# One ring of seven PSUM banks, value products of 6, 5 and 5 key tiles, and maxima turned by a matmul, in an attention and MLP kernel

## The chip, the cores and the metric

The kernel runs on one core of a Trainium2 chip. Five engines work beside each other and wait for each other through semaphores: TensorE (PE, matmuls; PEld is its loading of stationary operands), VectorE (DVE), ScalarE (ACT), GpSimd (POOL), and SyncE (SP), which issues the DMAs. Matmul results go to eight PSUM banks, each 128 partitions of 512 float32 numbers, from which DVE and ACT read them. The metric is the device time of one execution in microseconds (us); lower is better.

## The reference

```python
xn  = layernorm(x)                                   # x: 2048 x 1024
q, k, v = heads(xn @ wqkv)                           # 32 heads of 32 columns
p   = softmax(q @ k.T * 32 ** -0.5)                  # 2048 x 2048 for each head
s   = merge(p @ v) @ wo                              # 1024 x 1024
h   = xn @ w1 + b1                                   # 3584 columns
g   = silu((h * tanh(softplus(h))) @ w2)             # Mish between two dense layers
out = x + s * g
```

All of it is float32. The kernel splits most operands into a high and a low part in the type fp32r and takes three products (high by high, high by low, low by high); the products of softmax weights and values are in plain float32.

## The kernel before, in words

There are three stages. The first (to about 580 us) normalises `x`, makes values, queries and keys, and splits the MLP's weights. The third (from about 3295 us) is the output projection `op` (`p_mm`, L1073) with the end of the formula. Between them lies the long stage that the change is about, in which attention and MLP are woven into one another.

For each head, key tile `T` (128 keys, 16 to a head) and 512 queries, a matmul `t` (L748) makes scores with the row's maximum already subtracted: the stacked operands `qstack` and `kstack` hold three copies of 32 rows for the split, and two further rows of `qstack` hold the negated maximum as a high and a low part. ACT takes the exponential into an SBUF tile `p` (L756). POOL adds the 16 `p` tiles of a head one after the other into `z` (L777). TensorE multiplies them by the values (`pv`, L795) in four 32-column strips of its array, which gives all 2048 queries in one bank. Finally four matmuls `zp` (L818) sum `z` over its partitions, and `norm` divides.

The maxima come from another pass of the same scores, about five key tiles ahead: matmul `s` (L670), DVE's `reduce_max` `mx` (L676). After four query tiles `m_chain` (L686) reduces (`nm`), splits into high and low (`hl`, ACT then POOL), turns the 128x8 result by a TensorE transpose into 8x128 (`mtp`, L700), copies it to `mt` on ACT and has SP store it into `qstack` with two DMAs. A `t` waits for that.

The MLP supplies matmuls `h` (L893, 24 for one tile of 128 hidden columns by 512 rows) and `y` (L981, six to a bank), with a chain of ACT and DVE operations for Mish between them and DVE's additions `yacc` (L1001).

The engines' orders are written ahead of time by `Plan` (L74), which walks through the stage with durations of its own (`MM`, `PV` and the number in each `Op`), takes for each engine the ready operation with the lowest key, and emits it. `ring` objects stand for buffers: an operation may only be taken when each ring in its `take` has a free place. Banks are in fixed rings: `s` has two, `t` two (the turned maxima use these too), `d` three (`h`, `y`, Mish's `q` and `zp`), `o` one (`pv`). `p` has 5 tiles. An operation with `late` may be taken as soon as it is ready while TensorE is in column mode (`col`, its strips or the narrow transpose), and that many us later otherwise.

In words, a *visit* is below a run of TensorE instructions in strip form between instructions that use the whole array.

Of the kernel before, what the change touches and what calls it, by code (L numbers as in the profile page):

```python
# [9 lines left out]
F32 = mybir.dt.float32  # L10
# [52 lines left out]
class Op:  # L63


    def __init__(self, eng, took, need=(), emit=None, take=(), give=(), key=None, col=False, late=0.0,
                 bytes_=0, then=None, first=False, both=False):
        self.eng, self.took, self.need, self.emit = eng, took, need, emit
        self.take, self.give, self.key, self.col, self.late = take, give, key, col, late
        self.bytes, self.then, self.first, self.both = bytes_, then, first, both  # L70
        self.end = None


class Plan:  # L74
# [6 lines left out]
    SEM, SWITCH, LAND, RATE = 0.07, (0.2, 0.1), 2.0, 0.25e6  # L81
# [53 lines left out]
    def do(self, op, when):  # L135
# [27 lines left out]
    def run(self, streams):  # L163
        self.streams = [[s, None] for s in streams]
        while True:
# [5 lines left out]
            for e in sorted(left, key=self.at.get):  # L171
                now, best, soon = self.at[e], None, None
                for op in self.todo[e] + (heads if e == "PE" else []):
# [5 lines left out]
                    if "d" in op.take and not op.first and len(self.rings["d"]) == 1 and self.first_of("d"):  # L179
                        continue  # L180
# [3 lines left out]
                    key = (not op.late, r if op.key is None else op.key)  # L184
# [21 lines left out]
def body(ctx: ExitStack, tc: tile.TileContext, x, wqkv, wo, w1, b1, w2, out):  # L206
# [25 lines left out]
    make_identity(nc, ident)  # L232
    bias1 = consts.tile([P, FT], F32, name="bias1")
# [268 lines left out]
    stacks(early, 1)  # L502
    vt = {}

# [28 lines left out]
    def m_tail(h, g, mx):  # L533
        nm = early.tile([P, 4], F32, tag=f"nm{g % 2}", name=f"nm{h}_{g}")
        hl = early.tile([P, 2, 4], F32R, tag=f"hl{g % 2}", name=f"hl{h}_{g}")
# [9 lines left out]
        def r3():  # L545
            tp = ps1.tile([P, 512], F32, tag="ps", name=f"mtp{h}_{g}")
            nc.tensor.transpose(tp[:8, :P], hl.bitcast(F32).rearrange("p a b -> p (a b)"), ident)
            copy(mt, tp[:8, :P])
# [111 lines left out]
    def s_stream():  # L660
        for h in range(1, H):
            while h not in loaded:
                yield None
            for g in range(4):
                maxes, tiles = [], {}
                for qt in range(4 * g, 4 * g + 4):
                    for kc in range(4):
                        def mm(at, h=h, qt=qt, kc=kc, tiles=tiles):
                            tiles[qt, kc] = sp_ = bank("s", at["s"], f"s{h}_{qt}_{kc}")
# [3 lines left out]
                        def mx(at, h=h, g=g, qt=qt, kc=kc, tiles=tiles):  # L673
                            if qt == 4 * g and kc == 0:
# [4 lines left out]
                               emit=mm, take=["s"])  # L679
                        yield m  # L680
                        maxes.append(op("DVE", 0.69, need=[m] + maxes[:1], emit=mx, give=[("s", m)],
# [4 lines left out]
    def m_chain(h, g, maxes, tiles, late=LATE):  # L686
# [4 lines left out]
        def r2(at):  # L691
            tiles["hl"] = early.tile([P, 2, 4], F32R, tag=f"hl{at['hl']}", name=f"hl{h}_{g}")
            copy(tiles["hl"][:, 0], tiles["nm"])

        def r3(at):
            low(nc.vector if h == 0 else nc.gpsimd, tiles["hl"][:, 1], tiles["nm"], tiles["hl"][:, 0])

        def r4(at):
            tiles["tp"] = tp = bank("t", at["t"], f"mtp{h}_{g}")
            nc.tensor.transpose(tp[:8, :P], tiles["hl"].bitcast(F32).rearrange("p a b -> p (a b)"), ident)  # L700
# [13 lines left out]
        a = op("PE", 0.06, need=[a], emit=r4, take=["t"], give=["hl"], col=True, late=late)  # L714
        a = op("ACT", 0.28, need=[a], emit=r5, take=["mt"], give=[("t", a)])
# [3 lines left out]
    exps, adds, uses = {}, {}, {}  # L719
    vt_, pv, zs = {}, {}, {}  # L720
# [13 lines left out]
    def t_stream():  # L734
        pts = {}
        for T in range(NS):
# [4 lines left out]
            for c in range(4):  # L741
# [4 lines left out]
                def mm(at, T=T, c=c, h=h, kt=kt, tile_=tile_):  # L746
                    tile_[0] = tp = bank("t", at["t"], f"t{T}_{c}")
# [8 lines left out]
                m = Op("PE", MM, key=slot * (T + (c + 1) / 4), emit=mm, take=["t"],  # L756
                       need=[m_there[h, c]] if (h, c) in m_there else [])
                yield m
                exps[T].append(op("ACT", 0.69, need=[m] + exps[T][:1], emit=ex, take=["p"] if c == 0 else [], give=[("t", m)]))
# [8 lines left out]
            if kt % GROUP == GROUP - 1:  # L768
                product(T, pts)
# [17 lines left out]
    def product(T, pts):  # L787
        h, kt = divmod(T, NT)

        def emit(at):  # L790
            if kt == GROUP - 1:
                pv[h] = bank("o", 0, f"pv{h}")
            for k in range(kt - GROUP + 1, kt + 1):
# [4 lines left out]
        def then(o):  # L798
            for k in range(T - GROUP + 1, T + 1):
                p_done(k, o)  # L800

        need = [e for k in range(T - GROUP + 1, T + 1) for e in exps[k]]
        last_pv[h] = op("PE", PV * GROUP, key=slot * (T + 1.5), need=need + [vt_[h]], emit=emit, col=True,
                        take=["o"] if kt == GROUP - 1 else [], give=["v"] if kt == NT - 1 else [], then=then)
# [3 lines left out]
    def norm(h, product_, sum_):  # L808
# [6 lines left out]
        def z_mm(at):  # L815
            t["z"] = bank("d", at["d"], f"zp{h}")
# [26 lines left out]
        a = own = op("PE", 1.0, need=[sum_], emit=z_mm, take=["d"], give=["z"], col=True, late=LATE)  # L843
# [4 lines left out]
        a = op("DVE", 0.69, need=[a, oc], emit=n3, give=[("d", own)])  # L848
# [30 lines left out]
    def h_stream():  # L879
        for n in range(NC * FT):  # L880
# [7 lines left out]
            for k in range(KT):  # L888
                for a, b in THREE:
                    def mm(at, n=n, c=c, k=k, a=a, b=b, i=i, t=t):  # L890
                        if i == 0:
                            t["h"] = bank("d", at["d"], f"h{n}")
# [5 lines left out]
                           take=["d", "h"] if i == 0 else [],  # L898
# [8 lines left out]
    def mish(n, made, t):  # L907
# [9 lines left out]
        def a2(at):  # L917
            t["q"] = bank("d", at["d"], f"q{n}")
# [34 lines left out]
        p2 = op("ACT", 0.69, need=[p1], emit=a2, take=["d"], first=True)  # L953
# [5 lines left out]
        o5 = op("DVE", 0.69, need=[o4], emit=d5, give=[("d", p2)])  # L959
        o6 = op("DVE", 0.69, need=[o5, o3], emit=d6, give=["r"])  # L960
        p5 = op("ACT", 0.6, need=[o6], emit=a5, take=["act"])
        act_ops[n] = op("DVE", 0.69, need=[p5], emit=d7, give=[("d", t["own"]), "h"])
# [3 lines left out]
    def y_stream():  # L966
        for m in range(W2S):
            w2_op(m, [m_there[0, 3]])
        for B in range(NC * FT // YB):
            c, b = divmod(B, FT // YB)  # L970
            done = []
            for dh in range(2):
                for s in range(4):
                    t = {}
                    for j in range(YB):
                        n, m_ = YB * B + j, (B * 2 + dh) * YB + j
                        for i, (p, q) in enumerate(THREE):
                            def mm(at, n=n, m_=m_, p=p, q=q, s=s, i=i, j=j, dh=dh, B=B, t=t):
                                if j == 0 and i == 0:
                                    t["y"] = bank("d", at["d"], f"y{B}_{dh}_{s}")  # L980
# [4 lines left out]
                            while n not in act_ops or m_ not in w2_ops:  # L985
# [3 lines left out]
                                   need=[act_ops[n], w2_ops[m_]], take=["d"] if j == 0 and i == 0 else [], give=give)  # L989
# [12 lines left out]
                    done.append(op("DVE" if b else "ACT", 0.69 if b else 0.6, emit=y_add, give=[("d", t["own"])],  # L1002
# [67 lines left out]
    BANKS = ("s0", "s1", "t0", "t1", "d0", "d1", "d2", "o0")  # L1070
# [8 lines left out]
    def p_stream():  # L1079
# [31 lines left out]
        for part in range(2):  # L1111
            for n, name in enumerate(BANKS):
                t, dh = divmod(n, 2)
                need = {"s": "s", "t": "s", "d": "y" if name < "d2" else "z", "o": "z"}[name[0]]
                while need not in final:
                    yield None
                need = [final[need]] + ([last_t[H - 1]] if name[0] == "t" else [])
                for k in range(FIRST) if part == 0 else range(FIRST, KT):
                    for i in range(3):
                        def mm(at, t=t, dh=dh, k=k, i=i, name=name):  # L1120
                            if k == 0 and i == 0:
                                ps[t, dh] = bank(name[0], at[name[0]], f"op{t}_{dh}")
                            p_mm(t, dh, k, i)
                        yield Op("PE", MM, key=2 * total, need=need + [wo_ops[k], o_ops[k]], emit=mm,
                                 take=[name[0]] if k == 0 and i == 0 else [])
# [5 lines left out]
    m_chain(0, 3, [], {"mx": negm[0]}, late=0.0)  # L1131
# [49 lines left out]
    for c in range(NC):  # L1181
        for s in range(4):
# [3 lines left out]
            for dh in range(2):  # L1186
# [5 lines left out]
                if c:  # L1192
                    n = 2 * s + dh
                    ps[t, dh] = bank(BANKS[n][0], int(BANKS[n][1]), f"op{t}_{dh}")
# [38 lines left out]
```

## Time and profile before

| | |
|---|---|
| median of 3 runs | 3469.94 us (3468.89 to 3470.29) |
| the profiled execution | 3472.93 us, of which the span is 3471.2 us |
| PE busy | 3438.9 us, 99% |
| DVE, ACT, POOL busy | 2356.7, 1982.8, 2471.5 us |
| granted TensorE clock, mean | 0.999 |
| the woven stage | about 581 us (first `t`) to 3295 us (last `y`) |

A busy PE here isn't a TensorE that starts a matmul at every chance: a 128x512 matmul is recorded as 389 ns or more, while the next may start 227 ns after it. Where the distance from start to start is over 227 ns but the record still covers it, TensorE has lost time without an idle time being shown. So the profile is read below by starts and counts.

### The profile page before, as it was taken

What the parts mean: (1) busy time and instruction counts of PE and PEld (TensorE: products, weight loads), DVE (VectorE), ACT (ScalarE), POOL (GpSimd) and SP (SyncE); (2) the same over time, 40 slices, a digit from 0 to 9 for tenths busy, and PEclk for the clock granted to TensorE, in tenths of its full rate; (3) what the DMA queues carried; (4) which work ended last, traced back from release to release, by engine and by line L of the source; (5) the groups of instructions that cost most, each with busy time, mean ns of one, the idle gap of its engine ahead of it and who ended that gap; (6) DMA issues with size and microseconds to landing.
All of it is one profiled execution on the core that took longest, in us unless ns stands there. A gap on an engine that the chain in (4) does not pass through costs nothing.

```text
span 3471.2 us, 48388 instructions
## 1 busy us (share of the span) xinstructions
PE 3438.9 (99%) x17920; PEld 2519.7 (73%) x17920; DVE 2356.7 (68%) x3839; ACT 1982.8 (57%) x3298; POOL 2471.5 (71%) x846
## 2 busy tenths in 40 slices
PE   8999999999999999999999999999999999999999
PEld 8998887666666767677666676776666766766687
DVE  6012236877877777887887778778878788776533
ACT  6111112766666667666666667666666666667621
POOL 0654342788787878888878878888888788888800
PEclk9999999999999999999999999999999999999999
DMA  8898896433333354443343544343445433333382
GB/s 290 291 306 304 287 321 208 122 110 99 122 110 110 106 162 125 119 122 98 110 114 118 158 123 121 110 116 104 121 117 178 120 117 113 110 115 117 122 303 85
DMA packets 294192, 529.79 MB, mean 153 GB/s; under 512 B 88810, under 2 KB 147178, under 8 KB 270186
## 3 DMA queue, kind: packets, MB, share of 16 engines
q1 hardware_dynamic: 274100, 484.74, 45.1%
q10 hardware_dynamic: 19856, 41.95, 3.3%
q8 instruction: 142, 2.33, 0.3%
q14 instruction: 94, 0.77, 0.1%
HBM read 386.89 MB, written 138.67 MB: 151 GB/s over the span
## 4 chain that ended last, share of the span: by engine, by line
PE 94%; POOL 2%; DVE 2%; ACT 1%; DMA 1%; issue 0%; SPq 0%; POOLq 0%; ACTq 0%; DVEq 0%
PE h L893 17%; PE y L981 17%; PE t L748 13%; PE s L670 13%; PE pv L795 13%; PE qk L598 10%; PE v L312 5%; PE op L1076 5%; POOL z L777 1%; PE zp L818 1%; PE mtp L700 1%; DVE mx L676 1%; ACT p L252 1%; PE s L525 0%; PE pt L367 0%
## 5 line engine op out<-in xcount | busy, mean ns | idle before, releaser
L777 POOL TENSOR_TENSOR z<-z,p 128x2048 f32<-128x2048 f32 x448 | 2065.2, 4610 | 115.0 <-ACT p L252 92.2
L252 ACT ACTIVATE p<-t,zero 128x512 f32<-128x512 f32 x2048 | 1382.4, 689 | 516.2 <-PE t L748 495.6
L676 DVE TENSOR_REDUCE mx<-s 128x1 f32<-128x512 f32 x1984 | 1329.8, 686 | 396.1 <-PE s L670 390.8
L981 PE MATMUL y<-w,act 128*128 128x512 f32 x2688 | 865.7, 393 | 2.6 <-DVE r L938 1.9
L748 PE MATMUL t<-qstack,kstack 128*128 128x512 f32 x2048 | 807.0, 397 | 5.0 <-ACT p L252 3.5
L670 PE MATMUL s<-kstack,qstack 128*128 128x512 f32 x1984 | 779.1, 396 | 5.0 <-DVE mx L676 2.8
L893 PE MATMUL h<-xr,w 128*128 128x512 f32 x2016 | 698.5, 391 | 0.6 <-DVE yacc L1001 0.3
L981 PEld LDWEIGHTS y<-w,act 128*128 128x128 f32 x2688 | 501.6, 188 | 118.1 <-issue 5.0
L748 PEld LDWEIGHTS t<-qstack,kstack 128*128 128x128 f32 x2048 | 384.1, 188 | 117.9 <-ACT p L252 17.2
L795 PE MATMUL pv<-p,v 128*32 128x512 f32 x4096 | 466.0, 595 | 0.0
L670 PEld LDWEIGHTS s<-kstack,qstack 128*128 128x128 f32 x1984 | 372.3, 188 | 109.3 <-DVE mx L676 19.6
L893 PEld LDWEIGHTS h<-xr,w 128*128 128x128 f32 x2016 | 377.8, 188 | 82.1 <-issue 2.8
L598 PE MATMUL qk<-xc,qkw 128*128 128x512 f32 x1536 | 350.9, 389 | 0.0
L777 POOL TENSOR_TENSOR z<-p,p 128x2048 f32<-128x2048 f32 x32 | 147.6, 4612 | 262.3 <-PE zp L818 193.4
L1001 DVE TENSOR_TENSOR yacc<-yacc,y 128x512 f32<-128x512 f32 x416 | 283.2, 681 | 73.9 <-PE y L981 73.1
L598 PEld LDWEIGHTS qk<-xc,qkw 128*128 128x128 f32 x1536 | 288.1, 188 | 59.9
L795 PEld LDWEIGHTS pv<-p,v 128*32 128x32 f32 x4096 | 120.0, 109 | 274.5 <-issue 265.9
L893 PE MATMUL h<-xc,w 128*128 128x512 f32 x672 | 237.3, 392 | 0.2 <-DVE yacc L1001 0.2
L263 DVE TENSOR_TENSOR qst<-qk,qst 128x512 fp32r<-128x512 f32 x64 | 44.3, 692 | 245.9 <-ACT qst L255 245.9
L255 ACT ACTIVATE qst<-qk 128x512 fp32r<-128x512 f32 x64 | 38.3, 598 | 299.2 <-PE qk L598 264.6
L312 PE MATMUL v<-vw,xc 128*128 128x256 f32 x1536 | 191.4, 286 | 2.2 <-POOL vw L263 1.5
L312 PEld LDWEIGHTS v<-vw,xc 128*128 128x128 f32 x1536 | 187.3, 193 | 3.8 <-POOL vw L263 1.9
(90 smaller groups left out, 2385.0 us busy)
## 6 DMA issues: line engine op xcount, KB each, us to landing
w<-w1s SPq DMA_DIRECT2D x112, 1024.0 KB
w<-w2s SPq DMA_DIRECT2D x224, 512.0 KB
w2s<-pw SPq DMA_DIRECT2D x56, 512.0 KB
qstack<-qs SPq DMA_DIRECT2D x96, 256.0 KB
kstack<-ks SPq DMA_DIRECT2D x96, 256.0 KB
w1s<-w1p SPq DMA_DIRECT2D x20, 1024.0 KB
praw<-in_B_w_dram SPq DMA_DIRECT2D x72, 256.0 KB
x<-in_A_x_dram SPq DMA_DIRECT2D x32, 512.0 KB
```

The source lines that it names most:

```text
L252: nc.scalar.activation(out_, in_, fn, bias=zero if bias is None else bias, scale=scale)
L312: nc.tensor.matmul(ps[:, :256], xc[t // 4][:, a, k, (t % 4) * P:(t % 4 + 1) * P], w[:, b, k], start=n == 0, stop=n == 3 * KT - 1)
L598: nc.tensor.matmul(ps, w[:, a, k], xc[c][:, b, k], start=n == 0, stop=n == 3 * KT - 1)
L670: nc.tensor.matmul(sp_, qst[h % 3][:, qt * P:(qt + 1) * P], kst[h % 3][:, kc * 512:(kc + 1) * 512], start=True, stop=True)
L676: nc.vector.reduce_max(tiles["mx"][:, qt % 4, kc:kc + 1], tiles[qt, kc], axis=AX.X)
L748: nc.tensor.matmul(tp, kst[h % 3][:, kt * P:(kt + 1) * P], qst[h % 3][:, c * 512:(c + 1) * 512], start=True, stop=True)
L777: nc.gpsimd.tensor_tensor(zs[h], pts[T - 1] if kt == 1 else zs[h], pts[T], ALU.add)
L795: nc.tensor.matmul(pv[h][c * DH:(c + 1) * DH, :], vt[h][:, k, :], pts[T - kt + k][:, c * 512:(c + 1) * 512], start=k == 0, stop=k == NT - 1)
L893: nc.tensor.matmul(t["h"], w1t[n][:, a, k], xts_[c][:, b, k], start=i == 0, stop=i == 3 * KT - 1)
L981: nc.tensor.matmul(t["y"], acts[n][:, p, s * P:(s + 1) * P], w2t[m_][:, q], start=j == 0 and i == 0, stop=j == YB - 1 and i == 2)
L1001: nc.vector.tensor_tensor(ya, ya, t["y"], ALU.add)
L1076: nc.tensor.matmul(ps[t, dh], ohl[t // 4, k][:, a, s * P:(s + 1) * P], wt[k][:, b, r], start=k == 0 and i == 0, stop=k == KT - 1 and i == 2)
```

## The change

- Seven banks are one ring `b`, which `s`, `t`, `h`, `y`, `q`, `zp` and `mtp` all take from. The old rings stay as limits: at most 2 `s`, 2 `t`, 4 `d` at a time. The eighth bank stays with `pv`.
- A head's value product is in three pieces of 6, 5 and 5 key tiles instead of four pieces of 4. The last also needs POOL's finished sum (`adds[T]`), so that `zp` can follow it in the same visit. The `p` ring grows from 5 to 7 tiles, the `act` ring shrinks from 4 to 3. 15 KB a partition of DMA scratch are given up.
- The maxima are turned by an ordinary matmul in fp32r: the stationary operand is a fixed 128x128 tile `hl` whose first 8 columns hold the values and whose others are zero, the moving operand a 128x128 identity. It is no longer in strip form, and has `late` 4.0.
- The planner's durations change (`MM` 0.231 to 0.228, `PV` 0.91 to 0.86, `SWITCH` 0.2 and 0.1 to 0.25 and 0.13), an engine's next start may lie a little ahead of an end (`AHEAD`), and maxima and `y` additions get offsets in their keys (`urgent`).

```diff
-MM, PV = 0.231, 0.91
+MM, PV = 0.228, 0.86
-GROUP, YB = 4, 2
+GROUPS, YB = (6, 5, 5), 2
-LEAD, LATE = 5, 8.0
+LEAD, LATE = 5, 4.0
-PS, ACTS, W2S, Y0, Y1 = 5, 4, 5, 0.6, 0.17
+PS, ACTS, W2S, Y0, Y1 = 7, 3, 5, 0.6, 0.17
+S_B, T_B, D_B = 2, 2, 4
+U_MX, U_Y = -2.0, 1.0
...
+    AHEAD = {"DVE": 0.08, "ACT": 0.1, "POOL": 0.0}
-    SEM, SWITCH, LAND, RATE = 0.07, (0.2, 0.1), 2.0, 0.25e6
+    SEM, SWITCH, LAND, RATE = 0.07, (0.25, 0.13), 2.0, 0.25e6
...
             op.end = start + took
+            took -= self.AHEAD[e]
...
-                    key = (not op.late, r if op.key is None else op.key)
+                    key = (not op.late, r - op.urgent if op.key is None else op.key)
...
+    hls = [early.tile([P, P], F32R, name=f"hl{i}") for i in range(2)]
+    for t in hls:
+        nc.vector.memset(t.bitcast(F32), 0.0)
+    def parts(i):
+        return hls[i][:, :8].rearrange("p (a b) -> p a b", a=2)
+    def turn(tp, i):
+        nc.tensor.matmul(tp[:, :P], hls[i], ident_r, start=True, stop=True)
...
-    for name, n in (("s", 2), ("t", 2), ("d", 3), ("o", 1), ("p", PS), ("z", 1), ("e", 1), ("r", 1), ("on", 1),
+    for name, n in (("b", 7), ("s", S_B), ("t", T_B), ("d", D_B), ("o", 1), ("p", PS), ("z", 1), ("e", 1), ("r", 1), ("on", 1),
...
-    def bank(ring, i, name):
-        return ps_a.tile([P, 512], F32, tag=f"{ring}{i}", name=name)
+    def bank(at, name):
+        return ps_a.tile([P, 512], F32, tag=f"b{at['b']}", name=name)
...
-                               emit=mm, take=["s"])
+                               emit=mm, take=["s", "b"])
...
         def r4(at):
-            tiles["tp"] = tp = bank("t", at["t"], f"mtp{h}_{g}")
-            nc.tensor.transpose(tp[:8, :P], tiles["hl"].bitcast(F32).rearrange("p a b -> p (a b)"), ident)
+            tiles["tp"] = tp = bank(at, f"mtp{h}_{g}")
+            turn(tp, tiles["hl"])
...
-        a = op("PE", 0.06, need=[a], emit=r4, take=["t"], give=["hl"], col=True, late=late)
+        a = op("PE", 0.07, need=[a], emit=r4, take=["t", "b"], give=["hl"], late=LATE if h else 0.0)
...
-            if kt % GROUP == GROUP - 1:
-                product(T, pts)
+            if kt in group_of:
+                product(T, pts, group_of[kt])
...
+        if kt == NT - 1:
+            need.append(adds[T])
...
-        a = own = op("PE", 1.0, need=[sum_], emit=z_mm, take=["d"], give=["z"], col=True, late=LATE)
+        a = own = op("PE", 1.0, need=[sum_], emit=z_mm, take=["d", "b"], give=["z"], col=True, late=LATE)
```

What TensorE does at the end of a head, here head 15. `pv` is the value product, `zp` the partition sums, `mtp` a turned maximum, `s17_5_0` a score matmul for the maxima of head 17 and `t256_1` one for the weights of key tile 256 (head 16). Before, the last piece of the product and then, 40 rows further on, the sums:

```order
L670 MATMUL s17_5_0_18601<-kstack2_5380,qstack2_5379 128x512
L795 MATMUL pv15_17985<-p252_18409,v15_17764 32x512 x4
L795 MATMUL pv15_17985<-p253_18467,v15_17764 32x512 x4
L795 MATMUL pv15_17985<-p254_18499,v15_17764 32x512 x4
L795 MATMUL pv15_17985<-p255_18549,v15_17764 32x512 x4
L700 MATMUL mtp17_0_18628<-ident_154,hl17_0_18557 8x128
L981 MATMUL y26_0_3_18630<-w2_104_17840,act52_18104 128x512 x3
```

```order
L748 MATMUL t258_1_18730<-qstack1_2723,kstack1_2724 128x512
L670 MATMUL s17_7_1_18732<-kstack2_5380,qstack2_5379 128x512
L981 MATMUL y26_1_2_18706<-w2_107_18292,act53_18435 128x512
L818 MATMUL zp15_18736<-z15_17957,ones_164 32x512 x4
L893 MATMUL h55_18532<-xr1_12077,w1_55_18316 128x512
L981 MATMUL y26_1_3_18748<-w2_106_18147,act52_18104 128x512
```

After, the last piece and the sums:

```order
L1007 MATMUL y26_1_1_18579<-w2_107_18223,act53_18322 128x512
L691 MATMUL s17_6_1_18606<-kstack2_5383,qstack2_5382 128x512
L818 MATMUL pv15_18039<-p251_18307,v15_17702 32x512 x4
L818 MATMUL pv15_18039<-p252_18352,v15_17702 32x512 x4
L818 MATMUL pv15_18039<-p253_18383,v15_17702 32x512 x4
L818 MATMUL pv15_18039<-p254_18433,v15_17702 32x512 x4
L818 MATMUL pv15_18039<-p255_18483,v15_17702 32x512 x4
L844 MATMUL zp15_18634<-z15_17860,ones_166 32x512 x4
L1007 MATMUL y26_1_1_18579<-w2_107_18223,act53_18322 128x512
L919 MATMUL h55_18468<-xr1_12054,w1_55_18247 128x512
L771 MATMUL t257_2_18645<-qstack1_2725,kstack1_2726 128x512
```

The last piece has five key tiles instead of four, waits for POOL's sum, stands later against the `t` of the next head, and the sums come in the same visit.

The turning of one maximum on TensorE, the third of head 15. Before:

```order
L748 MATMUL t232_0_17368<-qstack2_5379,kstack2_5380 128x512
L893 MATMUL h50_17357<-xr1_12077,w1_50_17091 128x512 x2
L795 MATMUL pv14_17142<-p228_17160,v14_16930 32x512 x4
L795 MATMUL pv14_17142<-p229_17236,v14_16930 32x512 x4
L795 MATMUL pv14_17142<-p230_17287,v14_16930 32x512 x4
L795 MATMUL pv14_17142<-p231_17332,v14_16930 32x512 x4
L700 MATMUL mtp15_2_17403<-ident_154,hl15_2_17339 8x128
L670 MATMUL s15_13_0_17405<-kstack0_2718,qstack0_2717 128x512
L748 MATMUL t232_1_17409<-qstack2_5379,kstack2_5380 128x512
```

After (with line 523 the helper `turn`):

```order
L691 MATMUL s15_14_1_17380<-kstack0_2720,qstack0_2719 128x512
L919 MATMUL h50_17310<-xr1_12054,w1_50_17038 128x512 x2
L523 MATMUL mtp15_2_17386<-ident_r_159,hl1_2728 128x128
L691 MATMUL s15_14_2_17388<-kstack0_2720,qstack0_2719 128x512
L919 MATMUL h50_17310<-xr1_12054,w1_50_17038 128x512 x2
L771 MATMUL t233_2_17398<-qstack2_5382,kstack2_5383 128x512
L771 MATMUL t233_3_17401<-qstack2_5382,kstack2_5383 128x512
```

The turned maximum used to stand at the end of a visit; now it stands among whole-array matmuls with a load of 128 columns of its own.

The end of the woven stage on TensorE, where `y55` is the MLP's last block and `op0_0` the first tile of the projection. Before, with the sums of the last head:

```order
L981 MATMUL y55_0_2_31744<-w2_220_31541,act110_31531 128x512 x3
L981 MATMUL y55_0_2_31744<-w2_221_31670,act111_31685 128x512 x3
L981 MATMUL y55_0_3_31753<-w2_220_31541,act110_31531 128x512 x3
L981 MATMUL y55_0_3_31753<-w2_221_31670,act111_31685 128x512 x3
L981 MATMUL y55_1_0_31762<-w2_222_31679,act110_31531 128x512 x3
L1076 MATMUL op0_0_31767<-wo0_30236,xo0_31621 128x512 x3
L1076 MATMUL op0_0_31767<-wo1_30967,xo0_31621 128x512 x3
L1076 MATMUL op0_0_31767<-wo2_31609,xo0_31621 128x512 x3
L1076 MATMUL op0_0_31767<-wo3_31616,xo0_31621 128x512 x3
L1076 MATMUL op0_1_31787<-wo0_30236,xo0_31621 128x512 x3
L818 MATMUL zp31_31792<-z31_31156,ones_164 32x512 x4
L981 MATMUL y55_1_0_31762<-w2_223_31720,act111_31685 128x512 x3
```

After, with its last value product:

```order
L1007 MATMUL y54_1_3_31554<-w2_219_31321,act109_31400 128x512 x3
L1103 MATMUL op0_0_31567<-wo0_30128,xo0_31503 128x512
L1007 MATMUL y55_0_0_31570<-w2_220_31338,act110_31438 128x512 x3
L1103 MATMUL op0_0_31567<-wo0_30128,xo0_31503 128x512 x2
L818 MATMUL pv31_31112<-p507_31271,v31_30821 32x512 x4
L818 MATMUL pv31_31112<-p508_31316,v31_30821 32x512 x4
L818 MATMUL pv31_31112<-p509_31387,v31_30821 32x512 x4
L818 MATMUL pv31_31112<-p510_31433,v31_30821 32x512 x4
L818 MATMUL pv31_31112<-p511_31459,v31_30821 32x512 x4
L844 MATMUL zp31_31607<-z31_30998,ones_166 32x512 x4
L1007 MATMUL y55_0_0_31570<-w2_221_31514,act111_31579 128x512 x3
L1007 MATMUL y55_0_1_31626<-w2_220_31338,act110_31438 128x512 x3
```

The sums of the last head (`zp31`) used to be alone between `op` and `y`; now the last product and they stand together, four `y` tiles earlier.

More of the change, by code (lines that the diff above doesn't have):

```diff
@@ L178, in run @@
                         r = max(r, self.at["POOL"])
-                    if "d" in op.take and not op.first and len(self.rings["d"]) == 1 and self.first_of("d"):
+                    if not op.first and any(x in op.take and len(self.rings[x]) == 1 and self.first_of(x) for x in "db"):
                         continue
@@ L232, in body @@
     make_identity(nc, ident)
+    ident_r = consts.tile([P, P], F32R, name="ident_r")
+    nc.vector.tensor_copy(ident_r, ident)
     bias1 = consts.tile([P, FT], F32, name="bias1")
@@ L684, in s_stream, with m_chain @@
         final["s"] = m
-    def m_chain(h, g, maxes, tiles, late=LATE):
+    def m_chain(h, g, maxes, tiles):
         def r1(at):
@@ L847, in norm @@
         a = op("DVE", 0.69, need=[a], emit=n2, give=["r"])
-        a = op("DVE", 0.69, need=[a, oc], emit=n3, give=[("d", own)])
+        a = op("DVE", 0.69, need=[a, oc], emit=n3, give=[("d", own), ("b", own)])
         stored[h] = op("SP", 0.4, need=[a], emit=store, give=["on"], bytes_=P * 512 * 4)
@@ L952, in mish @@
         p1 = op("ACT", 0.73, need=[o1], emit=a1)
-        p2 = op("ACT", 0.69, need=[p1], emit=a2, take=["d"], first=True)
+        p2 = op("ACT", 0.69, need=[p1], emit=a2, take=["d", "b"], first=True)
         o2 = op("DVE", 0.75, need=[p1], emit=d2)
@@ L988, in y_stream @@
                             m = Op("PE", MM, key=tile_time * due, emit=mm,
[L989 removed]
+                                   need=[act_ops[n], w2_ops[m_]], take=["d", "b"] if j == 0 and i == 0 else [], give=give)
                             if j == 0 and i == 0:
```

79 lines of the change are left out of this document (41 added, 38 removed).

## The prediction

> **What bounds the kernel now.** I read the page first (sections 1, 2 and 4), then the woven stage by windows, then the timeline where TensorE changes its way of working, then the table of waits.
>
> ```profile
> span 3471.2 us, 48388 instructions
> PE 3438.9 (99%) x17920; PEld 2519.7 (73%) x17920; DVE 2356.7 (68%) x3839; ACT 1982.8 (57%) x3298; POOL 2471.5 (71%) x846
> PEclk9999999999999999999999999999999999999999
> PE 94%; POOL 2%; DVE 2%; ACT 1%; DMA 1%; issue 0%; SPq 0%; POOLq 0%; ACTq 0%; DVEq 0%
> ...
> 700.00:3200.00 2500.00, 2491.55 (x12861) 1734.09 (x12850) 1967.32 (x3177) 1672.37 (x2761) 2076.68 (x567) 1.00 0.40 119
> 700.00:3200.00 2500.00, 432.17 (x3804) 111.14 (x3792) 1.00 0.40 119
> 700.00:3200.00 2500.00, 30.89 (x232) 4.56 (x232) 1.00 0.40 119
> 700.00:3200.00 2500.00, 32.20 (x118) 9.81 (x118) 1.00 0.40 119
> ```
>
> TensorE carries 94% of the chain that ended last, with its clock granted at 0.9 or more in every slice. The four window rows are the stretch from 700 to 3200 us for everything, then for line 795 (`pv`), 818 (`zp`) and 700 (`mtp`) alone. So 12861 - 3804 - 232 - 118 = 8707 whole-array matmuls run there. What they need at least comes from these rows, of the chain and the timeline:
>
> ```profile
> 482.53 5.44 PE qk L598 x24
> 1099.40 0.13 PEld L795 LDWEIGHTS pv<-p,v 128*32 128x32 f32 x4 [0.30 <-issue]
> 1099.83 0.13 PEld L795 LDWEIGHTS pv<-p,v 128*32 128x32 f32 x4 [0.30 <-issue]
> ...
> 2201.52 0.39 PE L893 MATMUL h<-xr,w 128*128 128x512 f32 x1
> 2201.84 3.64 PE L795 MATMUL pv<-p,v 128*32 128x512 f32 x32
> 2205.41 0.73 PE L670 MATMUL s<-kstack,qstack 128*128 128x512 f32 x2
> ...
> 1353.20 0.61 PE L981 MATMUL y<-w,act 128*128 128x512 f32 x2
> 1353.75 1.06 PE L818 MATMUL zp<-z,ones 128*32 128x512 f32 x8
> 1354.74 0.50 PE L893 MATMUL h<-xr,w 128*128 128x512 f32 x1
> ...
> 1507.50 3.64 PE L795 MATMUL pv<-p,v 128*32 128x512 f32 x32
> 1511.07 0.27 PE L700 MATMUL mtp<-ident,hl 128*8 128x128 f32 x1
> 1511.10 0.48 PE L748 MATMUL t<-qstack,kstack 128*128 128x512 f32 x1
> ```
>
> A dense whole-array matmul costs 5.44 / 24 = 0.227 us; four strip instructions cost 0.43 us, so a key tile (eight) 0.86. A visit costs more than its content: from `h` at 2201.52 to `s` at 2205.41 are 3.89 us; less 0.227 for `h` and 8 x 0.43 = 3.44 for the product, 0.22 is left for the two changes of form. The `zp` visit, with its second `y` 0.227 after 1353.20, says the same: 1.31 - 0.227 - 0.86 = 0.22. A turned maximum at the end of a visit takes 0.03 (1511.07 to 1511.10).
>
> Sum for the stretch: 8707 x 0.227 = 1976; strips 4036 / 4 x 0.43 = 434; visits, 165 by the order of the whole stage and so some 153 here, x 0.22 = 34; 118 turned maxima x 0.03 = 4. That is 2448 of 2500 us. The other 52 us are waits, most too short to show as idle time (2500 - 2491.55 = 8.5 us). Over the whole stage I take 60.
>
> ```profile
> PEld s L670 <- DVE mx L676: 19.6, 42, 0.9
> PEld t L748 <- ACT p L252: 17.2, 42, 1.0
> ...
> 1500.38 0.39 PE L670 MATMUL s<-kstack,qstack 128*128 128x512 f32 x1
> 1500.81 0.69 DVE L676 TENSOR_REDUCE mx<-s 128x1 f32<-128x512 f32 x1 [0.61 <-PE s L670]
> ```
>
> The loads of `s` and `t` wait for the reader of the bank that they are to fill. From a matmul's start to its bank's release are 0.43 + 0.69 = 1.12 us, five matmul steps of 0.227. A bank refilled after five steps or fewer makes TensorE wait, one refilled after six barely doesn't.
>
> **The change, part by part.** *Visits.* In the order, 165 visits become 96: 32 fewer products, the sums inside the last, no maxima in strips. 69 x 0.22 = 15.2 us gained; the content of the visits is the same 512 key tiles.
>
> *Turned maxima.* 125 of them in the stage cost 0.03 now, 3.8 us. The new form isn't in the trace; its nearest rows are these:
>
> ```profile
> 119.84 4.36 PE L312 MATMUL v<-vw,xc 128*128 128x256 f32 x35
> 42.72 0.49 PE L367 MATMUL pt<-ident,x 128*128 128x128 f32 x3
> L700 PEld LDWEIGHTS mtp<-ident,hl x125: 82/83/124, 582.9 to 3171.9; 128*8 128x8 f32 x125
> L367 PEld LDWEIGHTS pt<-ident,x x128: 137/140/230, 9.2 to 69.6; 128*128 128x128 f32 x128
> ```
>
> 256 fp32r columns cost (4.36 - 0.28) / 34 = 0.12 and 512 cost 0.227, a line that ends at 0.067 for 128; that is the lower bound, as a matmul can't be free. `pt`, which loads 128 columns and moves 128, comes every (0.49 - 0.27) / 2 = 0.11. The upper bound is a full matmul, 0.227. I take 0.11, since `pt` has both sizes: 125 x 0.11 = 13.8, a loss of 10 us net (between 4.6 and 24.6). The Trainium skill, "TensorE: Matmul & The Clock Gate", section "LDWEIGHTS (loading the stationary operand)", has a rule that speaks against this part: a load lasts as many cycles of 1.2 GHz as the stationary operand has columns, so 107 ns for 128 and 7 for 8. The trace agrees only in direction, with 140 ns against 83; by the page's figure the new form would cost an estimated 125 x 0.107 = 13.4 us, which is no other sum. The copy to `mt`, the two DMAs of a maximum and their place on SP stay as they are.
>
> *Banks.* I laid both orders out by the bank that each tile takes, in steps of TensorE work. Before, 126 tiles go into a bank within five steps and 692 at six; after, 67 and 325. With 60 us of waits now, the tight reuses (818 to 392) would halve them if these were the cause of all, 30 us. If only those within five steps count, and each is one step short, it is 59 x 0.227 = 13 us; the waits that the rows above list are longer (36.8 us in 84, 0.44 each), but of PEld, whose waiting is partly hidden. I take 18, nearer to the row of the step; bounds 0 and 30. A loss isn't excluded and is priced as a rival below. The other distances in the order (last `h` to first `y`, reload of `w1` and `w2`, `mtp` to the `t` that needs it, 10 us at least) give no new wait, so the smaller `act` ring costs nothing: `y` starts 6.8 us or more of TensorE work after the `h` that it needs.
>
> *The product that waits for the sum.* All of TensorE is queued behind this wait, and with it ACT, DVE and POOL.
>
> ```profile
> 1500.16 0.39 PE L748 MATMUL t<-qstack,kstack 128*128 128x512 f32 x1
> 1500.58 0.69 ACT L252 ACTIVATE p<-t,zero 128x512 f32<-128x512 f32 x1 [0.67 <-PE t L748]
> 1567.32 23.32 POOL L777 TENSOR_TENSOR z<-z,p 128x2048 f32<-128x2048 f32 x5
> 1604.36 4.62 POOL L777 TENSOR_TENSOR z<-p,p 128x2048 f32<-128x2048 f32 x1 [9.01 <-PE zp L818]
> ```
>
> The last `t` of a head needs 0.42 + 0.69 + 4.66 (23.32 / 5) = 5.8 us until its sum is there, if POOL is free; the order puts 6.3 to 15.5 us of TensorE work between them (8 in the middle). From one `zp` to the next last product stand about 77 us of work, and POOL's 15 additions take 15 x 4.66 = 70: it has 7 us to spare, where now it idles 9 for `zp`. So I cost it at nothing, except for the last head, where the order has 67 us against 70: a wait of 3 us there.
>
> *The end.* That wait replaces others: the rows below show POOL adding without a pause and a wait for `wo`.
>
> ```profile
> 3206.97 4.62 POOL z L777
> 3253.91 4.63 POOL z L777
> PE op L1076 <- DVE wo L263: 1.8, 2, 1.6
> ```
>
> Ten steps of POOL lie between the two starts (46.94 us, 4.69 each), and `t` follows POOL there. After the change `op` with `wo2` stands some 5 us later behind the last `h`, so the 1.8 go; I take 2 us of gain for the end with the waits around it.
>
> *Sum.* -15.2 + 10 - 18 - 2 = -25 us. The profiled execution takes 3472.9 (span 3471.2 and 1.7 around it), so 3448; it lies 3.0 above the median of the runs, so 3445 there.
>
> **The rivals.** *(B) More gain.* The planner's numbers now fit the trace (0.228 for 0.227, 0.86 for 0.86), so waits fall by 30 and the turned maximum costs 0.067: 3445 - 12 - 5 = 3428. For it: tight reuses halve. Against: part of the waits have other causes, such as late DVE results. *(C) Dear maxima.* If 128 fp32r columns cost as much as 512 (+14.6) and waits fall by only 9 (+9), the time is 3469, no change. Nothing in the profile shows such a price. *(D) Slower: the last product waits for POOL.* POOL adds at 4.66 where the planner has 4.61, 0.7 us over 15 additions; at heads with 6.3 us of work against 5.8 that is already a wait, and a POOL one half addition behind makes it 2.3. With 1.6 us for each of 32 heads: 51 us, 3496. It decides from (25 + 7) / 32 = 1 us a head. Against: TensorE's own waits give POOL time. *(E) Banks give nothing:* -15.2 + 10 - 2 is 3463.
>
> In (D) a longer wait would cost twice, as this place shows:
>
> ```profile
> 1109.42 0.96 PE L981 MATMUL y<-w,act 128*128 128x512 f32 x3 [1.89 <-DVE r L938]
> 1106.00:1110.00 4.00, 2.11 (x11) 1.16 (x8) 3.97 (x7) 0.82 (x2) 3.52 (x1) 1.00 0.00 0
> 1110.00:1114.00 4.00, 4.00 (x12) 3.00 (x11) 2.70 (x6) 3.52 (x6) 3.92 (x2) 0.57 0.50 134
> ```
>
> After 1.89 us without a matmul the granted clock was 0.57 for the next 4 us, which costs 1.7 us more. The same page, section "Part 1: The HAM clock gate (the \"warmup\" mystery)", gives an idle window of about 3.4 us before the clock halves; by that (D)'s waits would never cost a clock, by the trace those near 1.9 us may.
>
> **How the numbers follow.** Chances: my forecast 0.45, (B) 0.17, (C) 0.15, (D) 0.15, (E) 0.08. Within 0.2% (6.9 us, about what a measurement can tell) is no change: that takes most of (C) and half of (E), 0.15; slower are (D) and the rest of (C), 0.19; faster 0.66. The range takes in (B), (C) and (E) with the bounds of the waits and maxima: 3418 to 3480; outside are most of (D) and the best of (B).
>
> **What would show it.** 96 visits and `zp` always straight after `pv`; the start of a matmul after `mtp` 0.11 us behind it (C: 0.2); PEld's waits of `s` for `mx` and of `t` for `p` well under 19.6 and 17.2 us; no row in which `pv` waits for POOL's `z`, except in the last head. (D) would show as waits of `pv` for POOL `z`, some 32 of over 1 us, and the prediction would be wrong if these, or new waits of `h` or `y` for DVE, exceed 25 us.

## The result, and the profile after

The changed kernel takes 3470.98 us (median; 3469.84 to 3476.82), the kernel before 3470.22 us in the same comparison (3468.89 to 3472.0). The ratio is 1.0005, with a 95% interval of 0.9998 to 1.0012: no change, where 3445 us were forecast. Four of the 20 runs of the changed kernel lie near 3476 us, at the same granted clock; the ratio includes them.

The page of the changed kernel, with its span, the engines' busy time and the chain that ended last:

```profile
span 3468.3 us, 48504 instructions
PE 3444.9 (99%) x17920; PEld 2548.3 (73%) x17920; DVE 2341.2 (68%) x3842; ACT 1970.8 (57%) x3298; POOL 2475.4 (71%) x846
PEclk9999999999999999999999999999999999999999
PE 97%; ACT 1%; DVE 1%; issue 0%; DMA 0%; POOL 0%; POOLq 0%; ACTq 0%
```

TensorE holds more of the chain than before (97% for 94%), at the same granted clock. Nothing here tells that anything was gained or lost. The same windows as in the prediction, 700 to 3200 us, for everything, for `pv` (now line 818), `zp` (844) and `mtp` (523):

```profile
700.00:3200.00 2500.00, 2495.86 (x12833) 1758.59 (x12835) 1957.76 (x3182) 1657.56 (x2758) 2070.62 (x563) 1.00 0.40 120
700.00:3200.00 2500.00, 423.31 (x3776) 113.69 (x3780) 1.00 0.40 120
700.00:3200.00 2500.00, 30.20 (x232) 7.54 (x232) 1.00 0.40 120
700.00:3200.00 2500.00, 27.09 (x118) 22.12 (x118) 1.00 0.40 120
```

There are again 12833 - 3776 - 232 - 118 = 8707 whole-array matmuls in 2500 us, exactly as many as before. By the forecast's prices they need 8707 x 0.227 = 1976, the strips 4008 / 4 x 0.43 = 431, some 90 visits 20, the maxima 118 x 0.06 = 7: 2434 us. So 66 us are lost in a stretch that lost 52 before, although the waits that were to fall have fallen. From the table of waits of the loads:

```profile
PEld t L771 <- ACT p L262: 7.5, 20, 1.4
PEld s L691 <- DVE mx L697: 6.0, 13, 0.9
```

They were 17.2 us in 42 waits and 19.6 us in 42. The steps that the forecast describes are there as well. The timeline of the changed kernel around a visit:

```profile
1505.86 0.39 PE L771 MATMUL t<-qstack,kstack 128*128 128x512 f32 x1
1506.09 0.39 PE L691 MATMUL s<-kstack,qstack 128*128 128x512 f32 x1
1506.32 0.22 PE L523 MATMUL mtp<-ident_r,hl 128*128 128x128 f32 x1
1506.38 0.68 PE L919 MATMUL h<-xr,w 128*128 128x512 f32 x2
1506.99 4.50 PE L818 MATMUL pv<-p,v 128*32 128x512 f32 x40
1511.30 1.04 PE L844 MATMUL zp<-z,ones 128*32 128x512 f32 x8
```

The next matmul starts 0.06 us behind `mtp`, and `zp` follows `pv` in one visit. But from `t` to `s` to `mtp` it is 0.23 each time, and counted over all starts in the stretch (distances up to 0.245 us, whole-array matmuls only) the mean distance went from 228.5 to 231.3 ns. It is clearest where nothing else happens, in the projection, which the change didn't touch. The kernel before, then the changed one:

```profile
3379.83 10.36 PE L1076 MATMUL op<-wo,xo 128*128 128x512 f32 x45
```

```profile
3379.65 10.52 PE L1103 MATMUL op<-wo,xo 128*128 128x512 f32 x45
```

Both are 45 matmuls without a gap. 44 distances take 10.36 - 0.39 = 9.97 us before, 226.6 ns each, and 10.13 us after, 230 ns each. The same instructions on the same shapes, with the clock at full speed in both, became 3.3 to 3.4 ns dearer; 2.8 ns x 8900 in the woven stage and 3.3 ns x 768 here are 27 us, the gain that is missing.

### The profile page after: what moved, and what is told of

The parts are those of the page before. It is cut to its first block, busy times and chain, and to the rows that moved or that the text cites. A ratio compares the mean times of both kernels' runs of the same rounds, so it can differ in the third digit from the quotient of the medians.

```text
span 3468.3 us, 48504 instructions
## 1 busy us (share of the span) xinstructions
PE 3444.9 (99%) x17920; PEld 2548.3 (73%) x17920; DVE 2341.2 (68%) x3842; ACT 1970.8 (57%) x3298; POOL 2475.4 (71%) x846
## 4 chain that ended last, share of the span: by engine, by line
PE 97%; ACT 1%; DVE 1%; issue 0%; DMA 0%; POOL 0%; POOLq 0%; ACTq 0%
PE h L919 18%; PE y L1007 18%; PE t L771 13%; PE s L691 13%; PE pv L818 13%; PE qk L619 10%; PE op L1103 5%; PE v L322 5%; PE zp L844 1%; ACT p L262 1%; PE s L546 0%; PE pt L377 0%; PE mtp L523 0%; DVE mx L697 0%; DMA vraw<-in_A_wqkv_dram 0%
## 5 line engine op out<-in xcount | busy, mean ns | idle before, releaser
L1007 PE MATMUL y<-w,act 128*128 128x512 f32 x2688 | 948.8, 395 | 0.2
L919 PE MATMUL h<-xr,w 128*128 128x512 f32 x2016 | 714.3, 395 | 1.5 <-ACT p L262 1.5
```

What stands on the lines that cost most here:

```text
L919: nc.tensor.matmul(t["h"], w1t[n][:, a, k], xts_[c][:, b, k], start=i == 0, stop=i == 3 * KT - 1)
L1007: nc.tensor.matmul(t["y"], acts[n][:, p, s * P:(s + 1) * P], w2t[m_][:, q], start=j == 0 and i == 0, stop=j == YB - 1 and i == 2)
```

## The experiments

**What the matmuls have in common.** In the addresses of the built programs one thing differs for all of these matmuls. Tiles are placed from the left end of SBUF (x, MLP weights, `act`, `p`) and from the right end (the score stacks, which the projection reuses for `wo`). The change takes two 32-byte tiles `hl` away on the right and puts two of 512 bytes there, 1024 - 64 = 960 bytes, which moves the stacks. The smaller DMA scratch moves the left tiles by another amount. Start addresses modulo 256: before, 192 on both sides; after, 192 left and 0 right. In the woven stage both operands of `s` and `t` lie on the right and both of `h` and `y` on the left, so there a matmul's own two operands always agree, and only the sides differ; in the projection three quarters of the `wo` operands lie on the right and the other operand on the left. Theory 1 was first put with 128 in place of 256, which fits these two as well. Theory 2 lays the dearer matmuls on the shared ring and its semaphore waits (625 instead of 453 instructions on TensorE only wait), theory 3 on the smaller scratch.

**1. The stacks back to the left tiles' place.** In the changed kernel:

```diff
-    pad = pool(ctx, "pad", 1, side="right").tile([P, 8], F32, name="pad")
+    pad = pool(ctx, "pad", 1, side="right").tile([P, 24], F32, name="pad")
```

> The changed kernel with the pad at the right end of SBUF grown from 32 to 96 bytes, so that the tiles placed from the right (the score stacks) start 64 bytes past a multiple of 128 again, as the tiles placed from the left do; nothing else moves. Theory 1 (places): matmuls come every 231 ns instead of 228.5 in the woven stage and 230 instead of 226.7 in the projection since the two groups of tiles no longer start at the same place within 128 bytes. Then some 8900 x 2.8 ns + 768 x 3.3 ns = 27 us go: 3443 us. Theory 2 (one ring): it is the shared ring with its additional semaphore waits on TensorE; then the time stays at 3471 and the distance at 231 ns.

3439.38 us, 0.9905 of the kernel before (0.989 to 0.992). The mean distance is 228.2 ns in the woven stage and 226.7 in the projection. 64 bytes of unused SBUF are worth 31 us, and the shared ring isn't what made matmuls dearer.

**2. The same step in the kernel before.** The same edit:

> The kernel before with the same longer pad, which puts the score stacks on a multiple of 128 bytes and leaves the left tiles 64 past one. Theory 1: matmuls in the woven stage go from 228.5 to about 231 ns and in the projection from 226.7 to 230: slower by some 25 us, 3495 us. Theory 2: no change, 3470 us.

3493.04 us, 1.0062 (1.0047 to 1.0077); 230.9 and 232.5 ns. The effect doesn't need the change.

**3. The left tiles moved instead.**

```diff
+    consts.tile([P, 16], F32, name="left_pad")
     one = consts.tile([P, 1], F32, name="one")
```

> The changed kernel with 64 bytes more at the left end, so that both groups of tiles start at a multiple of 128. If in theory 1 the two groups must only agree: 3443 us, as with the longer pad. If the place itself counts (64 past a multiple is the good one), everything is on the bad place and the first stage slows too (226.7 to 230 ns): above 3471 us. Theory 2: 3471 us, unchanged.

3435.57 us, 0.9901 (0.9885 to 0.9918), 228.2 and 226.7 ns, the first stage's 512-column matmuls at 226.7 as ever. So it isn't the place that counts but that both sides agree. This is the lowest median here, though not clear of the first and the eighth experiment, and it beats both kernels.

**4. The scratch alone, in the kernel before.**

```diff
-    nc = _bacc.Bacc("TRN2", target_bir_lowering=False, num_devices=1)
+    nc = _bacc.Bacc("TRN2", target_bir_lowering=False, num_devices=1, dynamic_dma_scratch_size=1024)
```

> The kernel before with the smaller DMA scratch of the changed one: all left tiles move down by 15360 bytes, a multiple of 128, and nothing else changes. Theory 1: no change, 3470 us and 228.5 ns. Theory 3 (the move by 15 KB, or the scratch itself, makes matmuls dearer): some 25 us slower, 3495 us.

3470.05 us, 0.9995 (0.9985 to 1.0006), 228.4 ns. Theory 3 falls.

**5. The change without the value stage's gain.** The longer pads also moved the value weights `vw`, and the 256-column value matmuls got faster with that, as 38 starts instead of 36 in the same 4.5 us show. The kernel of this experiment (the edit is below), where `vw` stays in its place, then the second experiment's:

```profile
119.75 4.48 PE L322 MATMUL v<-vw,xc 128*128 128x256 f32 x36
```

```profile
119.73 4.47 PE L312 MATMUL v<-vw,xc 128*128 128x256 f32 x38
```

To separate this, the changed kernel got its 64 bytes only behind the value stage:

```diff
+    pool(att0, "pad2", 1, side="right").tile([P, 16], F32, name="pad2")
     early = pool(att0, "early", 1, side="right")
```

> The changed kernel with 64 bytes inserted only from the score stacks on, after the value stage: stacks and left tiles start 64 past a multiple of 128, and the value weights vw stay where the kernel before has them. This takes the run with the longer pad (3439.4 us) apart: there vw had moved too, and the value matmuls came every 114.3 ns instead of 119.9. Theory 1: the change itself is worth what the forecast summed, and the value stage gave 1536 x 5.6 ns = 8.6 us on top: 3448 us, v at 119.9 ns, the woven stage at 228.2. If the value stage's gain is not from vw's place, 3439 us.

3441.31 us, 0.9918 (0.9903 to 0.9933), `v` at 119.9 ns, the woven stage at 228.1. So the change itself, with its matmuls at the old distance, is worth 29 us, and of the value stage's 8 us at most some 2 reach the end, which the runs don't tell from nothing. (In the first experiment `v` ends 8 us earlier, at 206.4 instead of 214.3 us, and `qk` then starts 2.5 us behind it instead of at once; at the first `t` 5.4 us are left, at the last `y` 0.3.) Its windows, in the order of those above:

```profile
700.00:3200.00 2500.00, 2495.26 (x12985) 1773.45 (x12984) 1963.87 (x3198) 1679.51 (x2794) 2090.26 (x569) 1.00 0.41 121
700.00:3200.00 2500.00, 430.64 (x3840) 115.56 (x3840) 1.00 0.41 121
700.00:3200.00 2500.00, 31.24 (x240) 7.80 (x240) 1.00 0.41 121
700.00:3200.00 2500.00, 27.18 (x118) 22.11 (x118) 1.00 0.41 121
```

8787 whole-array matmuls and 4080 strips: 1995 + 439 + 20 + 7 = 2461 us, so 39 us are lost where the kernel before loses 52 and the changed one 66.

**6. The value stage's gain without the change.** In the kernel before, the pad of the second experiment and another 64 bytes behind the value stage, so that the stacks are 128 bytes from where they were:

```diff
-    pad = pool(ctx, "pad", 1, side="right").tile([P, 8], F32, name="pad")
+    pad = pool(ctx, "pad", 1, side="right").tile([P, 24], F32, name="pad")
...
+    pool(att0, "pad2", 1, side="right").tile([P, 16], F32, name="pad2")
     early = pool(att0, "early", 1, side="right")
```

> The kernel before with vw on a multiple of 128 (the values' other operand xc stays 64 past one) and everything later where it was. If the value matmuls are the faster for their operands' different places: v at 114.3 ns, 3470.2 - 8.6 = 3461.6 us, and nothing else changes. If the gain in the value stage came with the changed kernel: 3470 us.

3494.27 us, 1.0068 (1.0053 to 1.0083). `v` is at 114.3 ns as foreseen, but the woven stage is at 231.1 and the projection at 232.0, although all large tiles start 64 past a multiple of 128. Theory 1 as it was put falls. What all runs so far share is the distance between right and left tiles modulo 256: 0 in the fast ones, 64, 192 and now 128 in the slow.

**7. and 8. 256 bytes.** In the kernel before `pad2` is 192 bytes instead of 64, which makes 256 with the pad; in the changed kernel the pad of the first experiment is longer by 256.

```diff
-    pool(att0, "pad2", 1, side="right").tile([P, 16], F32, name="pad2")
+    pool(att0, "pad2", 1, side="right").tile([P, 48], F32, name="pad2")
```

> The kernel before with vw moved by 64 bytes and everything placed from the right after the value stage moved by 256 instead of the 128 of the run that came out at 3494 us although all its tiles started 64 past a multiple of 128. The runs so far that kept 226.7 ns in the projection have right and left tiles a multiple of 256 bytes apart, the slow ones don't (distances mod 256: 0, 0, 0, 0 against 64, 192, 128). Theory 1a (agreement within 256 bytes): 228.5 ns in the woven stage, v at 114.3 ns, 3470.4 - 8.6 = 3462 us. If within 512 and only at half of it (all fast runs so far are 256 mod 512 apart): slow, 3494 us.

```diff
-    pad = pool(ctx, "pad", 1, side="right").tile([P, 8], F32, name="pad")
+    pad = pool(ctx, "pad", 1, side="right").tile([P, 88], F32, name="pad")
```

> The changed kernel with the longer pad made longer by 256 bytes more. Theory 1a: 3439 us as with the longer pad, 228.2 and 226.7 ns. If the distance has to be 256 mod 512: 3471 us, as the changed kernel.

3468.06 us (0.9991, 0.9981 to 1.0001) and 3437.76 us (0.9906, 0.9891 to 0.992). The projection in the sixth and in the seventh:

```profile
3379.74 10.60 PE L1077 MATMUL op<-wo,ohl 128*128 128x512 f32 x45
```

```profile
3379.81 10.36 PE L1077 MATMUL op<-wo,xo 128*128 128x512 f32 x45
```

128 bytes more on the right brought 226.6 ns back. Agreement modulo 256 bytes predicts the 512-column distances of all these runs. The expected 3462 us of the seventh were not reached: of the 8.6 us in the value stage some 3 arrive, and the interval of the ratio doesn't exclude none.

**9. The effect by itself.** In the kernel before, 64 bytes between the weights and the x tiles 1 to 3 of the first stage, where no attention runs:

```diff
+    pool(ph, "gap", 1).tile([P, 16], F32, name="gap")
     big = pool(ph, "big", 1)
```

> The kernel before with 64 bytes between the weights and the x tiles 1 to 3 of the first stage; x tile 0 stays. So in the query and key matmuls, which have no other work near them that could matter, three of four groups have operands that start 64 bytes apart within 256 and one group doesn't. Theory 1a, if it holds for the two operands of one matmul: 226.7 ns in the groups of tile 0, 230 to 233 ns in the others, 1152 x 4 ns = 5 us more; and the value matmuls of x tiles 1 to 3 at 114 ns instead of 120, 1152 x 5.6 ns = 6.5 us less: 3469 us together. If it needs matmuls with operands from different tiles in one stream (the woven stage): all 226.7 ns.

3472.24 us, 1.0002 (0.9992 to 1.0012). The query and key matmuls of the kernel before, then of this one, in the same place:

```profile
299.68 40.51 PE L598 MATMUL qk<-xc,qkw 128*128 128x512 f32 x178
```

```profile
299.77 40.46 PE L599 MATMUL qk<-xc,qkw 128*128 128x512 f32 x176
```

40.12 / 177 = 226.7 ns became 40.07 / 175 = 229.0. The matmuls come in groups: 24 of tile 0, whose operands agree, then 72 of tiles 1 to 3, whose operands are 64 bytes apart. One such change, with the first matmuls of tile 0, its last fourteen, and then sixteen of the others from the tenth on:

```profile
299.07 2.71 PE L599 MATMUL qk<-xc,qkw 128*128 128x512 f32 x11
301.39 3.33 PE L599 MATMUL qk<-xc,qkw 128*128 128x512 f32 x14
306.64 3.83 PE L599 MATMUL qk<-xc,qkw 128*128 128x512 f32 x16
```

From 299.07 to 301.39 are ten distances of 232 ns; behind them it is (3.33 - 0.39) / 13 = 226 ns for tile 0 and (3.83 - 0.39) / 15 = 229 for the others. Over all groups tile 0 has 231.0 ns in the first ten and 226.7 in the rest, tiles 1 to 3 have 230.8 and 228.9. So in a stream that keeps its places a matmul's own two operands decide, and a change of place makes some ten matmuls late on top of that, whichever way it goes. The whole time hardly moves, since the value matmuls of tiles 1 to 3 became faster (116.8 ns).

The changed kernel's own trace says the same of the woven stage. There the stream changes sides after at most four matmuls in 99 of 100 cases, so it is hardly ever ten matmuls from a change of place. Near its end, behind a `t`, 39 matmuls follow each other on one side:

```profile
3261.66 9.02 PE L1007 MATMUL y<-w,act 128*128 128x512 f32 x39
```

(9.02 - 0.39) / 38 = 227.1 ns, in a stage whose mean is 231.3. Over the whole stage two matmuls of one side have a mean distance of 231.3 ns within the first ten on that side and of 226.9 from the eleventh on; in the kernel before it is 228.4 and 226.9.

**10. The banks' freedom,** on the first experiment's kernel:

```diff
-S_B, T_B, D_B = 2, 2, 4
+S_B, T_B, D_B = 2, 2, 3
```

> The run with the longer pad (3439.4 us), and h, y, q and zp limited to three of the seven banks again, which with two for s and two for t gives each kind as many banks as before, though not fixed ones. If the freer banks brought the fall of TensorE's waits (40 us before, 29 after, of those over 18 ns): back to 40, 3451 us or more. If the planner's new numbers brought it: 3440 us.

3449.33 us, 0.994 (0.9925 to 0.9955): 10 us slower than with a fourth bank for these; 1 us of it is an estimate for five `zp` that stand alone again, at 0.22 a visit. The loads' waits for `mx` and `p` go back most of the way:

```profile
PEld t L771 <- ACT p L262: 15.2, 39, 1.0
PEld s L691 <- DVE mx L697: 15.0, 39, 0.9
```

**11. Value products of four key tiles,** on the same kernel:

```diff
-GROUPS, YB = (6, 5, 5), 2
+GROUPS, YB = (4, 4, 4, 4), 2
```

> The run with the longer pad (3439.4 us) with value products of four key tiles (four pieces a head), the last one still with the sums behind it. By the order 129 visits instead of 96. By the forecast's price 33 x 0.22 = 7 us slower: 3447 us. If visits are hidden or the ring of seven p tiles gives more slack: 3439 us.

3445.99 us, 0.9927 (0.9911 to 0.9944): 6.6 us slower. That this is near 7 is in part luck, since two other things moved and nearly cancel. A visit takes 0.22 us beyond its content in this trace as in the first experiment's, so the 33 visits did cost 7 us. Waits of over 18 ns fell from 29 to 21 us in the stretch. And 91 of the 125 maxima stand right behind a visit here, where there were 8:

```profile
1510.29 3.64 PE L818 MATMUL pv<-p,v 128*32 128x512 f32 x32
1513.86 0.33 PE L523 MATMUL mtp<-ident_r,hl 128*128 128x128 f32 x1
1514.02 0.45 PE L771 MATMUL t<-qstack,kstack 128*128 128x512 f32 x1
```

In that place the next matmul starts 0.16 us behind `mtp` and not 0.06; 83 more of these at 0.1 us take back the 8 us.

**12. The planner's old numbers,** on the same kernel:

```diff
-MM, PV = 0.228, 0.86
+MM, PV = 0.231, 0.91
-    AHEAD = {"DVE": 0.08, "ACT": 0.1, "POOL": 0.0}
+    AHEAD = {"DVE": 0.0, "ACT": 0.0, "POOL": 0.0}
-    SEM, SWITCH, LAND, RATE = 0.07, (0.25, 0.13), 2.0, 0.25e6
+    SEM, SWITCH, LAND, RATE = 0.07, (0.2, 0.1), 2.0, 0.25e6
-U_MX, U_Y = -2.0, 1.0
+U_MX, U_Y = 0.0, 0.0
```

> The run with the longer pad (3439.4 us) with the planner's old numbers (0.231, 0.91, changes of form 0.2 and 0.1, no start ahead of an end, no offsets in the keys). If the new numbers share in the fall of the waits: waits over 18 ns rise from 29 towards 40 us, 3450 us. If the banks brought it alone (with the old limit of three they rose to 36): 3440 us.

3495.89 us, 1.0068 (1.0053 to 1.0083), 56 us slower than with the new ones and far outside what was expected:

```profile
PEld t L771 <- ACT p L262: 46.8, 86, 1.6
PEld s L691 <- DVE mx L697: 12.5, 29, 1.3
PEld s L691 <- ACT p L262: 7.8, 17, 1.2
```

Waits of over 18 ns are 71 us in the stretch instead of 29. The mean granted clock of the profiled execution is 0.995, where the first experiment has 0.999; that is an estimated 0.004 x 3495 = 14 us at most. The last row is of a kind that the kernel before doesn't have: a maxima matmul waits for the exponential, whose banks it shares only in one ring. That a wrong order hurts more with one ring than with fixed ones is the nearest reading, but the old numbers were not run with fixed banks in the changed kernel, and which of the numbers does it wasn't taken apart.

## Why the prediction was wrong

*The step that failed* is the first price: "A dense whole-array matmul costs 5.44 / 24 = 0.227 us", measured in the first stage of the kernel before, and then used in the sum for both kernels as if no edit could move it. The new `hl` tiles were priced as an operation on TensorE and not as 960 bytes in front of the stacks. In its place the runs showed 231.3 ns instead of 228.5 in the woven stage and 230.0 instead of 226.7 in the projection, where the two sides no longer agree modulo 256. That cost 27 us by the distances and 30 us by the comparison of the fifth experiment with the changed kernel (3441.3 and 3471.0).

*The sum otherwise held.* With the matmuls at their old distance the change gives -29 us against the forecast -25, 3441 against 3445 us:

| term | forecast, us | measured |
|---|---|---|
| visits, 69 fewer | -15.2 | -15: their time beyond the content is 36.8 us before and 21.8 in the fifth experiment |
| turned maxima | +10 | +6: 3.8 us before, 10.0 in the fifth experiment |
| waits | -18 | about -13 of those over 18 ns (40.5 to 28.3 us in 2500), and some 4 more in shorter ones (228.5 to 228.1 ns) |
| the end | -2 | the rest, -3 |

The count of visits holds a small slip that doesn't show: ten of the 165 are a lone maximum, which costs 0.03 us and not 0.22.

*The turned maxima* were taken too dear: among whole-array matmuls `mtp` lies just under the lower bound of the forecast (0.067), the line through 512 and 256 columns, not on the row of `pt`; with waits and the eight behind a visit it is 0.08 on average. The Trainium skill, "TensorE: Matmul & The Clock Gate", section "Wait — 56ns, not 53.3ns?", has 55.6 ns for 128 columns between two starts; the trace's 0.06 us (1506.32 to 1506.38) agrees.

*The waits* fell as forecast, and for two reasons, of which the forecast had worked with one. The fourth bank that the ring gives `h`, `y`, `q` and `zp` is worth 10 us (experiment 10); with the planner's old numbers the changed kernel is slower than the kernel before even with its matmuls at the old distance (experiment 12). In the forecast these numbers stand only in rival (B).

*The product that waits for POOL's sum* costs nothing, as forecast: no start of a `pv` lies more than 0.43 us behind the matmul ahead of it, in the changed kernel and in the fifth experiment. The 3 us at the last head didn't come either. So (D) is out. The 3471 us look like (C), but (C)'s mechanism isn't there. *(E)* is refuted by experiment 10.

*What stays open.* Shown is that the operands' start addresses modulo 256, a matmul's own and those of the matmuls ahead, set the distance between matmuls. Not shown is which reads hinder each other, nor why ten matmuls pass before a change is forgotten. The Trainium skill, "TensorE: Matmul & The Clock Gate", section "Step-by-step: what each phase is for", says that TensorE has two independent read ports and that loading the next stationary operand takes no read bandwidth from the running matmul; by that alone, addresses shouldn't matter. The ninth experiment moved only the streamed operand against the stationary one and slowed the stream, which that sentence doesn't foresee; that the two reads collide is the nearest reading, but it is argued.

## What to carry to other kernels

When a change adds, drops or resizes any SBUF tile, compare the start addresses of the large matmul operands before pricing anything else: here both groups of operands had to be a multiple of 256 bytes apart, and a pad of 64 unused bytes decided over 30 us of 3470. A price per instruction that is read from one kernel holds for another only as long as addresses do; one uninterrupted row of equal matmuls in both profiles tells at a glance, if its operands come from both groups, as in the projection. And a planner that shares buffers between streams should have durations measured on the chip: here its old numbers came out as waits of one stream for another.

## What the runs showed of the hardware that was not expected

- In the projection a 512-column fp32r matmul comes every 226.7 ns if the start addresses of the two groups of tiles agree modulo 256 bytes, and every 230.0, 232.0 and 232.5 ns if they are 64, 128 and 192 apart, with a mean granted clock of 0.998 or more.
- For 256-column matmuls it is the other way round: 119.9 ns with agreement (192 and 192), 113.6 to 117.7 ns with `vw` 64 bytes below `xc` modulo 256. The eighth experiment has that same distance and 117.7 ns where the first has 114.3, so modulo 256 isn't the whole rule there.
- A change of place makes some ten matmuls late, 231 ns each, even where each one's own operands agree (experiment 9); a stream that changes sides every few matmuls never leaves this.
